# A lightning-attention and MoE kernel on one Trainium2 core: the second group of tokens without Strassen's scheme, weight sums moved to later steps, and the final row stored in parts

## The chip, the cores and the metric

The program runs on one NeuronCore of a Trainium2 chip. The metric is device time in microseconds of one execution, as the median of several. For each kernel one execution was also recorded by the hardware profiler; its span (first to last instruction) is about 1.8 us shorter than the time. Engines are named TensorE (PE in the profile; PEld are its weight loads), VectorE (DVE), ScalarE (ACT), GpSimd (POOL) and SyncE (SP).

## The reference

```python
# attention: B=4, H=8, S=768, D=64, in blocks of 64 rows, decay lam per head
for b in range(nb):
    intra = einsum(qb, kb) * Dmask[None];  intra = einsum(intra, vb)
    inter = einsum(qb * lam_pow, kv_state)
    out[:, :, sl] = intra + inter
    kv_state = lam_block * kv_state + einsum(kb * rev_pow, vb)
# then a dense layer on the 3072 tokens (d_model 512, d_ff 2048)
h = x @ w_in
g = 0.5 * h * (1 + tanh(c * (h + 0.044715 * h**3)))
return g @ w_out
```

Inputs and the output are float32; the matmuls run on float16 copies.

## The kernel before

Attention is done in 24 steps (0 to 23). Its output goes transposed into `xT`, in seven groups of tokens: group 0 has 512, groups 1 and 2 have 256 each, groups 3 to 6 have 512 each. For each group a list of pieces (`filler`) is queued, and `fill(n)` puts the next n pieces between parts of an attention step, so that TensorE always has dense work. A piece of the first layer (`mm1`) ends in a gelu on ScalarE, which writes `gT`. The second layer comes in two forms. `mm2` is the plain one. `product` is Strassen's scheme: seven half-size products in place of eight, for which VectorE makes sums of `gT` blocks (`gs`) and of `w_out` blocks (`w_sum`), and combines the products. Before the change, group 0 is plain and all others use the scheme.

```python
groups = [[0, 1], [2], [3], [4, 5], [6, 7], [8, 9], [10, 11]]
...
def sum_g(i0, i1):                       # five sums of gT on VectorE, one per product that needs one
    for m, ((T0, F0), op, (T1, F1)) in G_SUMS.items():
        if m not in gsum:
            ...                          # pairs live in the ring of four w32 buffers, with the raw weights
        pin(nc.vector.tensor_tensor(gsum[m][:, i, :], block(T0, F0, i), block(T1, F1, i), op))

def product(m, p):
    name, half = PLACE[m]
    if m in (3, 5, 1, 7):
        banks[name] = ps_M.tile([P, 2, HE], FP32, tag="M", name=f"M{name}")
    ...                                  # 8 matmuls of 256 columns into half a bank
    if m == 2:                           # A has 4 and 3, B has 5 and 2
        ...                              # two ScalarE copies of B, then two VectorE adds
    elif m == 1:
        pin(tt(d, banks["C"][:, 0].unsqueeze(1).to_broadcast([P, 2, HE]), d, ALU.add))
    elif m == 6:
        pin(tt(d, banks["D"][:], d, ALU.add))          # D has 7 and 6
        for T in range(2):               # two stores of 256 KB
            ...
...
if g == 0:
    ...                                  # plain
    return
...
for p in range(HN // P):
    for m in (3, 4, 5, 2, 1, 7, 6):
        filler.append(lambda m=m, p=p: product(m, p))
...                                      # sum_g is hung behind certain pieces, in two parts

# the program order around group 1
cast_wout(3, (POOL, ACT))
sum_wout(1, 3, DVE)                      # second half of the weight sums
fill(9)
prep(4)
sum_wout(1, 4, DVE)
stage_t(4)
...
sum_wout(1, 1, DVE)
fill(1); prep(8)
sum_wout(1, 7, POOL)
...
prep(9)
sum_wout(1, 6, POOL)
fill(2)
for n in range(8, NSTEP + 1):
    ...
    fill(2 if n <= 12 else 4)
    R(m, n - 1)                          # scores, products, mask, decay: the attention step
    fill(1)
    U(m)
    fill(2 if n in (8, 11) or n > 12 and n % 2 else 3)
```

## Time and profile before

| | before |
|---|---|
| median time, us | 214.4 (3 runs, 214.19 to 214.74) |
| span of the profiled run, us | 212.6 |
| TensorE busy | 93% |
| VectorE busy | 71% |
| mean granted clock of TensorE | 0.992 |

### The profile page before, as it was taken

How to read it: one execution, taken by the hardware profiler on the slowest of the kernel's cores; microseconds unless marked ns; L12 is line 12 of the kernel's file. 1: busy time of each engine (PE TensorE's matmuls, PEld its weight loads, DVE VectorE, ACT ScalarE, POOL GpSimd, SP SyncE). 2: the span in 40 equal slices, each digit the busy share in tenths (PEclk: the TensorE clock that was granted, in tenths of full speed). 3: DMA queues.
4: the chain of work that ended last, by engine and by line, in shares of the span. 5: the costliest groups of instructions: out<-in, count | busy, mean ns of one | idle time of the engine just before them, and what ended most of it. 6: DMA issues, size and time to landing. Idle time of an engine off the chain costs nothing.

```text
span 212.6 us, 5641 instructions
## 1 busy us (share of the span) xinstructions
PE 197.5 (93%) x2345; PEld 130.4 (61%) x2345; DVE 151.5 (71%) x282; ACT 108.0 (51%) x204; POOL 72.7 (34%) x82
## 2 busy tenths in 40 slices
PE   7788999799992999999999999999999999999990
PEld 2354544356882788855488845588654788445880
DVE  4988529987899978775999727996929773146631
ACT  2364778466770356467742377723376432565110
POOL 5494133646995253342341333044213100000000
PEclk9999999999999699999999999999999999999999
DMA  5999999999969588979695996664450003200022
GB/s 134 299 328 388 384 387 361 284 291 349 335 152 207 121 255 193 179 174 188 159 197 80 295 249 173 51 153 111 99 139 0 3 2 102 99 0 0 3 99 99
DMA packets 64297, 37.85 MB, mean 178 GB/s; under 512 B 17680, under 2 KB 59664, under 8 KB 64272
## 3 DMA queue, kind: packets, MB, share of 16 engines
q1 hardware_dynamic: 64272, 37.50, 68.5%
q8 instruction: 18, 0.29, 0.6%
q14 instruction: 7, 0.06, 0.1%
HBM read 27.27 MB, written 6.29 MB: 158 GB/s over the span
## 4 chain that ended last, share of the span: by engine, by line
PE 72%; DVE 13%; DMA 7%; issue 2%; SPq 2%; ACT 1%; DVEq 0%
PE Hps L401 30%; PE MB L466 8%; PE MD L466 8%; PE MA L466 7%; PE MC L466 4%; DVE w_sum L123 4%; DMA wo<-in_moe_w_out_dram 4%; PE Sps L271 4%; DVE gs L446 3%; PE OK L329 3%; DMA k<-in_k_dram 3%; PE OK L320 2%; PE O2ps L416 2%; SPq L68 2%; DVE qk L221 2%
## 5 line engine op out<-in xcount | busy, mean ns | idle before, releaser
L401 PE MATMUL Hps<-xT,w_in 128*128 128x512 f16 (+1 forms) x416 | 79.1, 346 | 0.0
L405 ACT ACTIVATE gT<-Hps 128x512 f16<-128x512 f32 x88 | 52.5, 596 | 26.4 <-PE Hps L401 25.6
L401 PEld LDWEIGHTS <-w_in 128*128 128x128 f16 x416 | 40.2, 98 | 33.3
L373 POOL TENSOR_TENSOR u<-t,lumask 128x256 f16<-128x256 f32 x40 | 29.3, 739 | 85.1 <-DVE t L366 65.6
L446 DVE TENSOR_TENSOR gs<-gT 128x512 f16<-128x512 f16 (+1 forms) x80 | 45.0, 627 | 11.8 <-ACT gT L405 11.6
L466 PEld LDWEIGHTS <-gs 128*128 128x128 f16 x400 | 39.1, 99 | 8.8 <-DVE gs L446 4.1
L280 DVE TENSOR_TENSOR PT<-Sps,mask 128x1024 f16<-128x1024 f32 x24 | 29.2, 1217 | 17.2 <-PE Sps L271 17.2
L211 POOL TENSOR_TENSOR v<-v,dv 128x512 f16<-128x512 f32 x24 | 29.1, 1214 | 4.8 <-DMA v<-in_v_dram 3.5
L343 ACT ACTIVATE xT<-OK 128x256 f16<-128x256 f32 x48 | 18.2, 452 | 20.0 <-PE OK L329 16.0
L473 ACT ACTIVATE m<-MB 128x512 f32<-128x512 f32 x10 | 6.0, 597 | 35.1 <-PE MB L466 35.1
L466 PE MATMUL MB<-w_out,gs 128*128 128x256 f16 x160 | 19.8, 277 | 3.8 <-DVE gs L446 3.8
L466 PE MATMUL MD<-w_sum,gs 128*128 128x256 f16 x160 | 20.2, 273 | 0.0
L226 ACT ACTIVATE qk<-k 128x512 f16<-128x512 f32 x24 | 15.0, 624 | 9.6 <-DMA k<-in_k_dram 9.6
L466 PE MATMUL MA<-w_sum,gT 128*128 128x256 f16 x160 | 19.5, 273 | 0.1
L221 DVE TENSOR_TENSOR qk<-q,dq 128x512 f16<-128x512 f32 x23 | 17.7, 768 | 0.0
L466 PEld LDWEIGHTS <-gT 128*128 128x128 f16 x160 | 15.5, 98 | 3.1 <-ACT gT L405 0.5
L477 DVE TENSOR_TENSOR o<-MA,m 128x512 f32<-128x512 f32 x10 | 6.9, 688 | 14.5 <-ACT m L473 14.5
L366 DVE SCALAR_TENSOR_TENSOR t<-t,lamu,OK 128x64 f32<-128x64 f32 x64 | 14.5, 273 | 2.1 <-PE OK L306 0.9
L416 PE MATMUL O2ps<-w_out,gT 128*128 128x512 f16 x64 | 14.6, 379 | 0.0
L271 PEld LDWEIGHTS <-qkT 64*64 64x64 f16 x384 | 6.3, 108 | 8.9 <-issue 4.4
L271 PE MATMUL Sps<-qkT 64*64 64x128 f16 x384 | 10.2, 226 | 1.0 <-DVE qkT L247 0.5
L123 DVE TENSOR_TENSOR w_sum<-wo,wo 128x1024 f16<-128x1024 f32 x6 | 8.0, 1362 | 4.2 <-DMA wo<-in_moe_w_out_dram 4.2
(53 smaller groups left out, 168.8 us busy)
## 6 DMA issues: line engine op xcount, KB each, us to landing
q<-in_q_dram SPq DMA_DIRECT2D x24, 256.0 KB, 4.4
k<-in_k_dram SPq DMA_DIRECT2D x24, 256.0 KB, 4.9
v<-in_v_dram SPq DMA_DIRECT2D x24, 256.0 KB, 5.0
out_dram<-o SPq DMA_DIRECT2D x24, 256.0 KB, 3.3
wo<-in_moe_w_out_dram SPq DMA_DIRECT2D x4, 1024.0 KB, 9.1
wi<-in_moe_w_in_dram SPq DMA_DIRECT2D x4, 512.0 KB, 7.7
wi<-in_moe_w_in_dram SPq DMA_DIRECT2D x2, 1024.0 KB, 12.2
qkT<-qk SPq DMA_TRANSPOSE x15, 4.1
```

The costliest lines, as they stand in the source:

```text
L123: pin(eng.tensor_tensor(w_sum16[:, w_slot[m], 4 * j : 4 * j + 4, :], a[:, :, e0 * HE : e0 * HE + HE], b[:, :, e1 * HE : e1 * HE + HE], op))
L211: pin(nc.gpsimd.tensor_tensor(wide(tv[:]), ld32[s][2][:], decay(dv, s), ALU.mult))
L221: pin(q_eng.tensor_tensor(wide(tq), q32[:], decay(dq, s), ALU.mult))
L271: pin(nc.tensor.matmul(Sps[half64(c), hl, hp, jk, :], o[half64(hl), 1, jk, hp, half64(c)], o[half64(hl), 0, :, hp, half64(c)], start=True, ...
L280: pin(nc.vector.tensor_tensor(t[:].rearrange("p a b c d -> p (a b) (c d)"), Ss.pop(n)[:].rearrange("p a b c d -> p (a b) (c d)"), mask[:]. ...
L343: pin(nc.scalar.activation(out=dst[:, :, c * P : (c + 1) * P].rearrange("p hp (t j) -> p hp j t", j=2), in_=OK[c][:, 0:256].rearrange("p ( ...
L373: pin(nc.gpsimd.tensor_tensor(u[:], state[half][:].unsqueeze(2).to_broadcast([P, 2, 2, D]), lumask[:, 2 * half : 2 * half + 2, :].unsqueez ...
L401: pin(nc.tensor.matmul(by_block(Hps[:, i, :]), w_in16[:, c, f * P : (f + 1) * P], x(c), start=(c == 0), stop=(c == NC - 1)))
L405: pin(nc.scalar.activation(out=dst, in_=Hps[:], func=AF.Gelu_apprx_tanh))
L416: pin(nc.tensor.matmul(O2[tau][0][:], gT[:, f % HF, f // HF, tau * P : (tau + 1) * P], w_out16[:, f, :], start=(n == 0), stop=(n == NF - 1)))
L446: pin(nc.vector.tensor_tensor(gsum[m][:, i, :], block(T0, F0, i), block(T1, F1, i), op))
L466: pin(nc.tensor.matmul(dst, lhsT, rhs, start=(i == 0), stop=(i == HF - 1), skip_group_check=True))
```

## The change

The intent: group 1 comes while VectorE has the least room, and its `gs` sums hold up TensorE. Group 1 goes back to the plain form, which needs no sums. Then the second half of the weight sums is first needed by group 2, so those five sums leave the crowded stretch and are done on VectorE in steps 8 to 10. Separately, the last row of the output is stored in three parts, each as soon as it is done.

```diff
+            final = g == len(groups) - 1 and p == HN // P - 1
+            if final and m == 6:
+                name = "E"
-            if m in (3, 5, 1, 7):
+            if m in (3, 5, 1, 7) or name == "E":
...
+            elif final and m in (7, 6):
+                o, T = banks["o"], (0 if m == 7 else 1)
+                row = row0 + T * HN + p * P
+                rows = out[row : row + P, :].rearrange("q (e d) -> q e d", e=2)
+                if m == 7:
+                    low = row0 + HN + p * P
+                    pin(nc.sync.dma_start(out=out[low : low + P, 0:HE], in_=o[:, 0, 1, :]))
+                d = o[:, T, T, :]
+                pin(tt(d, banks[name][:, half], d, ALU.add))
+                if m == 7:
+                    pin(nc.scalar.dma_start(out=rows, in_=o[:, :, 0, :]))
+                else:
+                    pin(nc.sync.dma_start(out=rows[:, 1], in_=d))
...
+        if g == 1:
+            for tau in range(NTAU):
+                for part in (0, 2, 1, 3):
+                    filler.append(lambda tau=tau, part=part: mm2(tau, part))
+            return
...
-    sum_wout(1, 3, DVE)
-    sum_wout(1, 4, DVE)
-    sum_wout(1, 1, DVE)
-    sum_wout(1, 7, POOL)
-    sum_wout(1, 6, POOL)
...
-        fill(2 if n in (8, 11) or n > 12 and n % 2 else 3)
+        for p in {8: (3, 4), 9: (1, 7), 10: (6,)}.get(n, ()):
+            sum_wout(1, p, DVE)
+        fill(2 if n == 11 or n > 12 and n % 2 else 3)
```

## The prediction

> **What bounds the kernel now.** I began with the page: the busy shares and the 40 slices.
>
> ```profile
> PE 197.5 (93%) x2345; PEld 130.4 (61%) x2345; DVE 151.5 (71%) x282; ACT 108.0 (51%) x204; POOL 72.7 (34%) x82
> ...
> PE   7788999799992999999999999999999999999990
> ...
> PEclk9999999999999699999999999999999999999999
> ```
>
> TensorE is busy for 93% of a span of 212.6 us, so the kernel as a whole is bound by its matmuls. But one slice near 64 to 69 us falls to 2, and the next one has a clock of 6 tenths. The waits of TensorE, asked first for the stretch 38 to 92 us and then for 92 us to the end, say how much can be won:
>
> ```profile
> PE MB L466 <- DVE gs L446: 3.8, 1, 3.8
> PE Tps L242 <- DVE qk L221: 1.3, 1, 1.3
> PE Sps L271 <- DVE qkT L251: 0.3, 1, 0.3
> ```
>
> (total us, times, longest). After 92 us the answer is empty: from there to the tail only the number of matmuls counts, and any time won before 92 us is kept unless it runs into a transfer. The timeline of VectorE and GpSimd around the long wait shows its cause:
>
> ```profile
> 60.49 5.61 DVE L446 TENSOR_TENSOR gs<-gT 128x512 f16<-128x512 f16 x5
> 66.02 1.21 DVE L280 TENSOR_TENSOR PT<-Sps,mask 128x1024 f16<-128x1024 f32 x1
> 67.16 0.84 DVE L366 SCALAR_TENSOR_TENSOR t<-t,lamu,OK 128x64 f32<-128x64 f32 x4
> 67.92 3.27 DVE L446 TENSOR_TENSOR gs<-gT 128x512 f16<-128x512 f16 x5
> ...
> 56.06 2.36 POOL L123 TENSOR_TENSOR w_sum<-wo 128x1024 f16<-128x1024 f32 x1
> ...
> 61.43 2.54 POOL L123 TENSOR_TENSOR w_sum<-wo 128x1024 f16<-128x1024 f32 x1
> ```
>
> Five sums of gT for group 1 (the second group of tokens) take 5.6 us, while their median is 0.42 us. One of them lasts 2.57 us, from 61.67 us, beside the 2.54 us GpSimd weight sum. The second five start only at 67.92 us, and TensorE, which has done half of product 5, waits for the first of them. Windows of one microsecond then show the granted clock:
>
> ```profile
> 69.50:70.50 1.00, 1.00 (x6) 0.51 (x4) 1.00 (x2) 0.00 (x0) 0.74 (x1) 0.50 1.13 272
> 70.50:71.50 1.00, 1.00 (x45) 0.89 (x48) 1.00 (x4) 0.78 (x2) 0.00 (x0) 0.50 0.00 0
> 71.50:72.50 1.00, 1.00 (x22) 0.77 (x15) 1.00 (x3) 0.33 (x2) 0.00 (x0) 0.50 0.00 0
> ```
>
> The figure after the five engines is the clock: 0.50 for some 3 us after the stall, so the stall is paid for twice.
>
> **What the skill says.** (1) "SBUF — State Buffer", § Who interferes with whom: a VectorE instruction with two SBUF inputs contends with a GpSimd instruction that reads SBUF. The trace agrees: 2.57 us for a sum whose median is 0.42, beside the GpSimd sum. (2) "TensorE: Matmul & The Clock Gate", Part 1: after about 3.4 us idle the clock falls to half, and about as much work brings it back. The trace agrees: a 3.79 us gap, then 0.50. (3) "VectorE: DVE Perf Modes", § The TRN2 errata: an fp32 tensor_tensor takes (N+151)/0.96 ns; N=1024 gives 1.22 us, and the undisturbed weight sums took 1.21 to 1.22. (4) "SBUF — State Buffer", § The DMA setup-cost knee: a transfer pays about 2 us that do not depend on its size. The last 256 KB stores land 2.5 to 2.6 us after issue, which fits.
>
> **The change part by part.**
>
> *Group 1 loses Strassen's scheme.* Removed: 7 products of 8 matmuls of 256 columns. A run of 8 takes 0.873 us (MA x8, 0.87 in the chain), so 7 x 0.873 = 6.11 us. Added: 2 tiles of 16 matmuls of 512 columns; a run of 8 takes 1.73 us (O2ps x8), so 4 x 1.73 = 6.92 us. On TensorE the change costs **+0.8 us**, all on the path. What it buys is that these matmuls need only gT from ScalarE: the ten gs sums (8.9 us of VectorE in this stretch) and the four combining adds (4 x 0.68) go away. ScalarE gets two copies of 0.60 us instead of 0.60 + 0.38; it is 51% busy, so nothing.
>
> So the wait on gs goes: **-3.79 us**. The slow clock goes too. From 68.64 to 73.56 us TensorE did 12 matmuls of MB, one attention step, and 8 of MC. At full clock this is 12 x 0.109 + 1.03 (the same step from 84.42 to 85.45) + 0.87 = 3.21 us instead of 4.92: **-1.7 us**.
>
> *Weight sums moved.* Five sums of the second half (products 3, 4, 1 on VectorE, 7 and 6 on GpSimd) become five VectorE sums in steps 8 to 10, where group 2 is their first reader. Two of the old ones stood ahead of the first attention preparation, around 38.74 us (2.05 us) and 42.16; that preparation's qk ended at 42.23, and TensorE waited 1.30 us for it although its earlier work ended at 40.99. Without the sum, qk can run from 38.74 to about 39.7, and k is done at 40.05 (ScalarE, 39.42 + 0.63), both before TensorE is free: **-1.3 us**. The sum of 1.25 us at 52.93 stood ahead of the copy for which TensorE waited at 55.86: **-0.3 us**.
>
> The new places cost VectorE 2.4, 2.4 and 1.2 us. My estimate of a step from the same matmul pieces: one attention step 0.93, six pieces of 0.87, together 6.1 us. VectorE has in step 8: mask 1.22, decay about 0.9, sums 2.44, next q 0.68, together 5.3 us; step 9 the same; in step 10: 0.68 + 1.22 + 0.9 + 1.22 and the first five gs sums of group 2 (2.6), together 6.6. That last is over by 0.5 us, but before, group 2 had product 5 start at 86.16 with its first sums done at 83.17 and the second at 85.9, and the second half of the product needs them only after 86.6. I take this for hidden. The staging buffers are reused in a ring of four, and gs of group 2 now takes the ones of the weights; all their readers are in order on VectorE ahead of it, so no new wait.
>
> *The final row.* Before: the last matmul ends near 207.3, an add of 128x512 runs from 207.42 to 208.11, and SP issues two stores of 256 KB from 208.14 to 209.34, one after the other. The second is issued at about 208.7 and lands 2.5 us later; the span ends 1.4 us after that. After: the product 7 half is added first. It stands behind the MC add (begun 206.64, spacing 0.60), so at about 207.24; at (256+151)/0.96 = 0.42 us each, with about 0.33 us between starts, the last add ends near 208.0. The last store of 128 KB is issued then, at once, with the 256 KB row store 0.3 us ahead of it on ScalarE's queue and the third store long gone. Last issue 208.0 instead of 208.7, and a little less to move behind it: **-0.9 us**.
>
> **Sum:** +0.8 - 3.8 - 1.7 - 1.3 - 0.3 - 0.9 = -7.2 us, and 214.4 - 7.2 = 207.2. I add 0.1 for small new waits: **207.3 us**.
>
> **The rivals.**
>
> *The wait moves to group 2.* VectorE is late with the five sums, so gs of group 2 makes TensorE wait. For: step 10 is slightly over full, and GpSimd's v and u work can stretch a 1.22 us sum to 2 (it did at 38.74, 2.05). Against: VectorE loses some 16 us of work between 38 and 76 us (8.9 gs, 2.7 adds, 4.5 of sums) and gets 6.1 back, and GpSimd loses 4.9. It would give back 1 to 3 us; a gap over 3.4 us would also bring back the slow clock, and the time would be near 212.
>
> *DMA becomes the bound from 38 to 65 us.* For: the DMA share there is 1.0 to 1.1 at 280 to 350 GB/s, k for step 5 was waited for until 42.06, and the 7 us won mean that the same bytes must come sooner. Against: later loads were not waited for at all in this stretch, they are asked for three steps ahead, and land in about 5 us. It would take back 0.5 to 2 us: 208 to 209.5.
>
> *The gap was partly hidden.* If something else, such as the transposing transfer for the next step, had stopped TensorE soon after in any case, less than 5.5 us comes back. Against: after the stall no wait of TensorE is left in the trace, although it then ran close behind its inputs.
>
> *The stores in parts wait for each other.* If the row's parts were ordered as one buffer, the last add would wait 2.5 us for a store to have read it. The parts are disjoint, so I give this little; it would make the tail 2 us longer.
>
> **Range and chances.** The stall with its slow clock (5.5) is the safest term; the 0.8 is sure; the 1.3 and 0.9 could each be half. The best case without losses is about 206.0; a new wait of 2 us gives 209.3. Range 206.0 to 209.3. Faster by over 2% means below about 210.2; that fails only if a new wait of 3 us appears: 0.91. Within 2%: 0.08. Slower: 0.01.
>
> **What would show it.** The waits of TensorE between 38 and 92 us should be empty or under 0.5 us; the clock 1.00 in every slice after the start; O2ps matmuls rise from 64 to 96 and those on gs fall from 400 to 360; the first preparation's transposes start at 41.0 instead of 42.3; TensorE ends near 201 us instead of 207.3; the time from its end to the span's end shrinks from 5.3 to about 4.4 us. A wait of MB on gs near 78 us, or one on qkT or k, would make the prediction wrong.

## More of the kernel before

The 71% of VectorE is an average. The windows view of the kernel before, in stretches of 4 us, gives the length of the stretch, then for each engine busy us and, in brackets, the number of instructions, in the order PE, PEld, DVE, ACT, POOL; then the granted clock, the DMA share and GB/s:

```profile
58.00:62.00 4.00, 4.00 (x85) 3.44 (x83) 3.90 (x7) 3.18 (x7) 4.00 (x5) 1.00 0.63 141
62.00:66.00 4.00, 2.85 (x26) 2.14 (x23) 4.00 (x4) 1.40 (x3) 3.15 (x2) 1.00 1.39 228
66.00:70.00 4.00, 1.36 (x10) 1.14 (x11) 4.00 (x9) 0.00 (x0) 2.31 (x3) 0.93 0.84 206
70.00:74.00 4.00, 4.00 (x70) 3.08 (x68) 4.00 (x7) 1.64 (x4) 0.24 (x1) 0.65 0.36 77
```

VectorE is the third figure pair: 15.9 of 16 us. Where TensorE stands still (2.85 and 1.36 of 4 us), VectorE is full, and in 62 to 66 us it gets through only four instructions, beside a sum on GpSimd.

## The result, and the profile after

| | before | after |
|---|---|---|
| median time, us | 214.57 (4 runs, 214.19 to 215.48) | 207.5 (4 runs, 207.16 to 209.66) |
| span of the profiled run, us | 212.6 | 205.6 |
| last matmul ends, us | 207.39 | 200.57 |
| from there to the end, us | 5.21 | 5.03 |
| TensorE busy | 93% | 96% |
| mean granted clock over the span | 0.992 | 1.000 |

The ratio is 0.9686, with a 95% interval of 0.9613 to 0.9759. A ratio is the mean time of one kernel's fast runs over that of the other's fast runs of the same rounds, so it is not quite the ratio of the medians quoted here. One of the four runs of the kernel after, 209.66 us with a mean clock of 0.990, is apart from the other three (207.16 to 207.61). It has no trace, and its cause is open.

The page of the kernel after has the same three rows as were shown of before: the busy shares, TensorE in 40 slices, and the granted clock.

```profile
PE 197.1 (96%) x2321; PEld 128.0 (62%) x2321; DVE 144.4 (70%) x271; ACT 108.1 (53%) x204; POOL 69.9 (34%) x80
...
PE   7988999999999999999999999999999999999990
...
PEclk9999999999999999999999999999999999999999
```

The dip and the slow slice are gone. TensorE's waits over the whole execution (total us, times, longest) are these:

```profile
PE idle L573 <- DVE ones L144: 1.5, 1, 1.5
PE Hps L514 <- DVE w_in L107: 0.8, 1, 0.8
PE Sps L271 <- DVE qkT L247: 0.5, 1, 0.5
PE Tps L242 <- DVE qk L221: 0.3, 1, 0.3
PE OK L320 <- DVE t L366: 0.2, 1, 0.2
```

All five also come up when only the first 21 us are asked for. The stretch from 36 to 86 us, and that from 86 us to the end, list none. So the three waits that the prediction listed are gone, and none has taken their place.

VectorE, however, has not become free. The windows of the kernel after, one for each attention step from step 8 on and the last for step 11, have the same columns as above:

```profile
58.70:64.80 6.10, 6.10 (x79) 3.38 (x78) 5.99 (x9) 3.08 (x6) 5.21 (x4) 1.00 1.25 241
64.80:71.00 6.20, 6.20 (x89) 4.28 (x88) 6.20 (x9) 2.96 (x6) 4.06 (x4) 1.00 1.12 274
71.00:77.50 6.50, 6.44 (x93) 5.44 (x92) 6.50 (x11) 4.76 (x10) 2.94 (x3) 1.00 1.12 247
77.50:82.90 5.40, 5.40 (x85) 4.66 (x84) 4.71 (x11) 2.16 (x5) 1.53 (x2) 1.00 0.90 155
```

VectorE is busy for 18.7 of the 18.8 us of steps 8 to 10. It is full and TensorE still never waits for it. How near that is to a new stall is a question for the experiments.

At the tail, the timeline of the kernel before shows one add for both halves and two stores, issued one after the other:

```profile
207.42 0.69 DVE L484 TENSOR_TENSOR o<-MD,o 128x512 f32<-128x512 f32 x1
208.14 1.20 SPq L487 DMA_DIRECT2D out_dram<-o  x2
```

and that of the kernel after has two adds and three stores, the first of them (not shown) at 199.93:

```profile
199.53 1.04 PE L469 MATMUL ME<-w_sum,gs 128*128 128x256 f16 x8
199.82 0.68 DVE L484 TENSOR_TENSOR o<-MC,o 128x512 f32<-128x512 f32 x1
...
200.61 0.42 DVE L494 TENSOR_TENSOR o<-MD,o 128x256 f32<-128x256 f32 x1
200.95 0.41 DVE L494 TENSOR_TENSOR o<-ME,o 128x256 f32<-128x256 f32 x1
201.06 0.64 ACTq L496 DMA_DIRECT2D out_dram<-o  x1
201.39 0.36 SPq L498 DMA_DIRECT2D out_dram<-o  x1
```

The matmuls of product 7 are done near 199.7, but its add begins at 200.61: 0.79 us after the start of the add ahead of it, whose result it reads (it is also 0.04 us after the end of the last matmul, 200.57; the run with another order of products, below, tells the two apart). The last add ends 0.79 us after the last matmul (201.36 against 200.57). Before it was 0.72 (208.11 against 207.39). The parts have not brought the last add forward at all.

### The profile page after: what moved, and what is told of

The parts are those of the page before. It is cut to its first block, busy times and chain, and to the rows that moved or that the text cites. A ratio compares the mean times of both kernels' runs of the same rounds, so it can differ in the third digit from the quotient of the medians.

```text
span 205.6 us, 5583 instructions
## 1 busy us (share of the span) xinstructions
PE 197.1 (96%) x2321; PEld 128.0 (62%) x2321; DVE 144.4 (70%) x271; ACT 108.1 (53%) x204; POOL 69.9 (34%) x80
## 4 chain that ended last, share of the span: by engine, by line
PE 91%; DVE 2%; DMA 2%; issue 1%; ACT 1%; DVEq 0%
PE Hps L401 35%; PE O2ps L416 10%; PE MB L469 8%; PE MA L469 7%; PE MD L469 7%; PE Sps L271 4%; PE MC L469 4%; PE Hps L514 4%; PE OK L329 3%; PE idle L573 3%; PE OK L320 3%; PE Tps L242 2%; DMA qkT<-qk 2%; PE OK L306 1%; DVE t L366 1%
## 5 line engine op out<-in xcount | busy, mean ns | idle before, releaser
L373 POOL TENSOR_TENSOR u<-t,lumask 128x256 f16<-128x256 f32 x40 | 31.4, 791 | 80.9 <-DVE t L366 54.2
L446 DVE TENSOR_TENSOR gs<-gT 128x512 f16<-128x512 f16 (+1 forms) x70 | 36.6, 586 | 10.8 <-ACT gT L405 10.6
L469 PEld LDWEIGHTS <-gs 128*128 128x128 f16 x360 | 34.9, 98 | 4.0
L416 PE MATMUL O2ps<-w_out,gT 128*128 128x512 f16 x96 | 21.9, 379 | 0.0
L221 DVE TENSOR_TENSOR qk<-q,dq 128x512 f16<-128x512 f32 x23 | 19.2, 834 | 0.0
L469 PE MATMUL MA<-w_sum,gT 128*128 128x256 f16 x144 | 17.5, 273 | 0.1
L469 PE MATMUL MD<-w_sum,gs 128*128 128x256 f16 x136 | 17.5, 273 | 0.0
L469 PE MATMUL MB<-w_out,gs 128*128 128x256 f16 x144 | 17.2, 273 | 0.0
L480 DVE TENSOR_TENSOR o<-MA,m 128x512 f32<-128x512 f32 x9 | 6.2, 688 | 13.9 <-ACT m L476 13.9
L469 PEld LDWEIGHTS <-gT 128*128 128x128 f16 x144 | 14.0, 98 | 2.8 <-ACT gT L405 0.3
L416 PEld LDWEIGHTS <-gT 128*128 128x128 f16 x96 | 9.2, 98 | 9.9
```

Of the source, the lines that this page charges most:

```text
L221: pin(q_eng.tensor_tensor(wide(tq), q32[:], decay(dq, s), ALU.mult))
L373: pin(nc.gpsimd.tensor_tensor(u[:], state[half][:].unsqueeze(2).to_broadcast([P, 2, 2, D]), lumask[:, 2 * half : 2 * half + 2, :].unsqueez ...
L416: pin(nc.tensor.matmul(O2[tau][0][:], gT[:, f % HF, f // HF, tau * P : (tau + 1) * P], w_out16[:, f, :], start=(n == 0), stop=(n == NF - 1)))
L469: pin(nc.tensor.matmul(dst, lhsT, rhs, start=(i == 0), stop=(i == HF - 1), skip_group_check=True))
```

## The experiments

Three questions were open. What did each part bring? Was the stall caused by contention with GpSimd or by the amount of VectorE's work, and what did the slow clock cost by itself? And why did the tail give 0.2 us and not 0.9? All runs gave correct results. The kernel before was run again on the chip of each set: 214.63, 214.44 and 215.18 us (medians of 11 runs each). Times from the last matmul to the end are good to 0.05 us, as the spans are given to 0.1; the first expectation writes 5.29 and 5.05 us for what is 5.21 and 5.03 here.

### The parts by themselves

**Only the final row in parts** (the kernel before with the tail edits of the diff above and nothing else).

> The kernel before with only the final row stored in parts. My prediction gave this part 0.9 us. The trace of the changed kernel speaks for less: from the end of the matmuls to the end of the span it has 5.05 us against 5.29 before. Theory (the last adds are chained on VectorE, so that the last store is not issued earlier; only the second issue and some bytes are saved, and the end of the program costs a little more with a second store queue): 0.2 to 0.4 us faster than before, the stall of 3.8 us unchanged. Rival (0.9 is right and the one trace is an accident): 0.8 to 1.0 us faster, with 4.4 us from the last matmul to the end.

Measured: 213.58 us against 214.63. This can't be read from the times, because the runs of before on this chip go from 212.86 to 215.51 (see below). In the trace it has 4.63 us from the last matmul to the end against 5.21, and the stall of 3.8 us is there as before. That 0.6 us lies between the two theories. Runs of like mean clock on this chip say about the same: three of before at 0.990 to 0.992 have 214.25 to 214.49, five of this one at 0.991 to 0.992 have 213.48 to 214.30, with medians 0.7 us apart.

**Everything but the final row in parts** (the changed kernel without the tail edits).

> The changed kernel with the old way of storing the final row. If the tail is worth 0.2 to 0.4 us, this is 0.2 to 0.4 us slower than the changed kernel, 6.5 to 6.9 us faster than before, and about 5.3 us from the last matmul to the end. If it is worth 0.9, it is only 6.1 us faster than before.

Measured: 207.52 us (6 runs, 207.17 to 207.79), ratio 0.9669, and 5.03 us from the last matmul to the end. The changed kernel has 207.5 us and 5.03 us as well. Between these two the tail edit is worth nothing that shows. Over all traces with the old tail (before, this one, and three experiments below) the time from the last matmul to the end is 5.21, 5.03, 5.01, 5.16 and 5.18, mean 5.12. Over those with the new tail (after, its repeat, tail only, and three experiments below) it is 5.03, 4.99, 4.63, 5.05, 5.02 and 5.07, mean 4.97. The means differ by 0.15 us, and by 0.09 without the trace of the tail alone. So the edit is worth nothing in one pair of kernels and 0.6 to 0.7 us in the other; the section on the prediction takes this up.

**Only group 1 made plain**, with the weight sums left in their old places:

```diff
+        if g == 1:
+            for tau in range(NTAU):
+                for part in (0, 2, 1, 3):
+                    filler.append(lambda tau=tau, part=part: mm2(tau, part))
+            return
-        fill(2 if n in (8, 11) or n > 12 and n % 2 else 3)
+        fill(2 if n == 11 or n > 12 and n % 2 else 3)
```

> The kernel before with only the second group of tokens made dense; the weight sums stay where they were, two on GpSimd. Theory (my terms: stall 3.79 and slow clock 1.71 go, 0.81 of matmuls is added, the waits of 1.30 and 0.32 us for VectorE sums at 42 and 56 us stay): 4.7 us faster than before, TensorE waits of 1.3 and 0.3 us still there, clock 1.00. Rival (the moved sums were needed to take the stall away, because GpSimd's two long sums hold up VectorE just there): a wait of 1 us or more remains between 60 and 75 us and the gain is below 4 us.

Measured: 209.5 us, 5.1 us below the median of before (ratio 0.9761, from 0.9722 to 0.9801, so "unclear" by the 2% rule, but clearly faster). Its TensorE waits between 30 and 60 us are the two that the sums cause, and there is none later:

```profile
PE Tps L242 <- DVE qk L221: 1.1, 1, 1.1
PE Sps L271 <- DVE qkT L251: 0.3, 1, 0.3
```

So the stall goes even with the two GpSimd sums in place: plain matmuls read nothing that VectorE makes. Moving the sums is worth the rest, 209.5 - 207.52 = 2.0 us. The prediction had 1.3 + 0.3 for it.

### What the stall was made of

**Matmuls of ones in the gap** (the kernel before, with TensorE kept busy while it waits):

```diff
+        if g == 1:
+            k5 = len(filler) - 5
+            five = filler[k5]
+            filler[k5] = lambda: (idle(16), five())
```

> The kernel before with 16 matmuls of ones (16 x 0.216 = 3.45 us at full clock) put into the gap in which TensorE waits for the sums of gT; nothing else is changed and the sums come no earlier. Theory (the slow clock after the gap is a cost of its own of 1.7 us): the clock stays at 1.00 and the kernel is 1.7 us faster than before although it does 3.5 us more of matmuls. Rival (after the gap TensorE would be held by VectorE's sums anyway, so that the clock costs nothing): same time as before within 0.4 us, with new waits on the sums or the mask.

Measured: 212.91 us against 214.63, which is 1.7 us faster although TensorE does 3.5 us more. In its timeline the matmuls of ones fill the gap, and product 5 goes on at 68.62 where it went on at 68.64 before:

```profile
64.23 3.62 PE L555 MATMUL idle<-ones 128*128 128x512 f16 x16
67.69 0.60 PE L466 MATMUL MB<-w_out,gs 128*128 128x256 f16 x4
68.62 1.49 PE L466 MATMUL MB<-w_out,gs 128*128 128x256 f16 x12 [0.34 <-DVE gs L446]
```

and its windows after the gap have the clock at 1.00:

```profile
70.00:72.00 2.00, 2.00 (x63) 1.77 (x63) 2.00 (x5) 1.64 (x4) 0.22 (x1) 1.00 0.25 61
```

The next attention step starts 1.55 us earlier than before (76.31 against 77.86). The slow clock is a cost of its own.

The same cost explains a part of the spread of the kernel before. Sorted by the mean clock, its 33 runs in the three sets fall into classes:

| mean clock | runs | time, us |
|---|---|---|
| 0.998 | 2 | 212.72 to 212.86 |
| 0.990 to 0.992 | 11 | 214.12 to 214.55 |
| 0.985 to 0.986 | 6 | 214.18 to 214.66 |
| 0.977 to 0.978 | 14 | 215.02 to 216.18 |

(The one of 216.18 counts as slow by being over 1.5% above the fastest; it is not in the ratios.) The two runs that kept the clock are as fast as the kernel with the gap filled. This correlation covers all 33 runs; I did not control what decides how long the slow phase lasts. The mean clock is a rough guide, though, as it also counts the time after the last matmul: the trace of the kernel with only group 1 plain has a mean of 0.995, yet in its windows the clock is below 1.00 only from 205 us on, and its last matmul ends at 202.79. That may be why the two middle classes have the same times; no trace of the class at 0.985 was kept.

**The two GpSimd sums on VectorE** (the kernel before; `sum_wout(1, 7, POOL)` and `sum_wout(1, 6, POOL)` with `DVE`).

> The kernel before with only one thing changed: the two weight sums that GpSimd did at 56 and 61 us are done by VectorE at the same places of the program. Theory (the stall comes from too much VectorE work in front of the second five sums of gT; the contention with GpSimd is only a part): VectorE gets 2.4 us more and gives back about 3 us of stretched sums, so the second five begin 0 to 1 us earlier, TensorE still waits 2.8 to 4 us, and the time is 0 to 1 us better (up to 2.5 if the gap becomes short enough that the clock stays up). Rival (the contention with GpSimd is the stall): the wait falls below 1 us and the time is 4 us or more better.

Measured: 213.61 us against 214.44, 0.8 us faster, at the edge of the noise (ratio 0.9965, from 0.9929 to 1.0). With GpSimd's long sums gone, the first five `gs` sums do take 2.60 us in place of 5.61. But the two sums now stand in VectorE's own queue, and the second five start later than before, at 68.39 (67.92 before):

```profile
66.76 0.60 PE L466 MATMUL MB<-w_out,gs 128*128 128x256 f16 x4
69.09 1.48 PE L466 MATMUL MB<-w_out,gs 128*128 128x256 f16 x12 [1.72 <-DVE gs L446]
...
63.94 2.60 DVE L446 TENSOR_TENSOR gs<-gT 128x512 f16<-128x512 f16 x5
...
68.39 3.25 DVE L446 TENSOR_TENSOR gs<-gT 128x512 f16<-128x512 f16 x5
```

Product 5 goes on at 69.09, 0.45 us later than before. The wait of 1.72 us is shorter only because TensorE now also waits 2.3 us for a copy of qkT near 58 us. In this run the two shorter stops leave the clock at 1.00 in every window from 64 to 76 us, and the first-layer piece after the products starts at 74.05 where it was 75.14: the 0.45 us lost are won back with 1.1 us to spare by the faster matmuls. (Its three other runs have mean clocks of 0.986 to 0.991 and no trace, so whether the clock stayed up in them is not shown. The two runs of before that kept the clock, 212.72 and 212.86, are faster than this one's 213.40.) My expectation that the second five would start 0 to 1 us earlier missed. The rival (contention is the stall) misses by far more: what fills VectorE is the amount of work, and moving it between the two engines only moves the stop.

### The price of leaving the scheme out, and the room that is left

**Group 2 made plain too** (`if g in (1, 2):`).

> The changed kernel with the third group of tokens (256 tokens too) made dense as well. No wait of TensorE stands there any more, so this measures the price of leaving out the scheme by itself. Theory: 32 x 0.216 - 56 x 0.109 = 0.81 us, all on the path: 0.7 to 0.9 us slower than the changed kernel. Rival (the scheme's price on VectorE still delays something hidden): same time or faster.

Measured: 208.15 us (207.69 to 209.67) against 207.5 of the changed kernel, 0.65 us slower and slightly below the range. The trace says how much. Its attention step near 71 us starts 0.30 us late by the start of the run (71.34 against 71.04), and its last matmul ends 0.86 us late (201.43 against 200.57), so the edit costs 0.56 us of TensorE's time. In the changed kernel, the first product of group 2 takes longer than its 1.04:

```profile
76.34 1.27 PE L469 MATMUL MA<-w_sum,gT 128*128 128x256 f16 x8
```

It needs the last gelu of its group at once, while the plain form starts with older ones. If that is the cause, which no run here shows, these 0.23 us come back, and 0.81 - 0.23 = 0.58.

**Two of the moved sums done twice** (`{8: (3, 4), 9: (1, 7, 7), 10: (6, 6)}`), run beside the unaltered changed kernel.

> The changed kernel, unaltered, on the same chip as the next three, as their measure. 207.2 to 207.7 us; from the last matmul to the end 4.8 to 5.1 us.

> The changed kernel with two of the moved weight sums done twice (the same values written again), one more in step 9 and one more in step 10: 2.4 us more of VectorE work ahead of group 2's sums of gT. Theory (VectorE is full from 59 to 77 us in the changed kernel, 18.7 of 18.8 us, and the second half of product 5 has only about 1.4 us of room): TensorE waits about 1 us for the sums of gT near 80 us, and the kernel is 0.7 to 1.5 us slower than the changed kernel. Rival (there is ample room, as my prediction had it with 5.3 us of work in steps of 6.1): no wait, same time within 0.2 us.

Measured: the changed kernel again has 207.43 us, and this one 208.53, 1.1 us slower. The stall is back, at group 2:

```profile
79.39 0.60 PE L469 MATMUL MB<-w_out,gs 128*128 128x256 f16 x4
80.74 1.48 PE L469 MATMUL MB<-w_out,gs 128*128 128x256 f16 x12 [0.75 <-DVE gs L446]
```

So by my estimate (2.4 us of work added, a wait of 0.75 us) the changed kernel stands 1 to 2 us of VectorE work away from the same stall, one group later.

**The sums for products 7 and 6 on GpSimd**, in the same steps 9 and 10 (`POOL if p in (7, 6) else DVE`).

> The changed kernel with the moved sums for products 7 and 6 on GpSimd instead of VectorE, at the same places in steps 9 and 10. Theory (the engine does not matter here as long as group 2's sums come in time, and GpSimd's long sums stretch VectorE's by about what they save it): time within 0.4 us of the changed kernel, perhaps a wait of up to 1 us on the sums of gT near 80 us. Rival (having the sums on VectorE is a part of the gain): 1.5 us or more slower.

Measured: 207.42 us against 207.43, and no TensorE wait after 36 us. The five `gs` sums of group 2 take 4.82 us beside GpSimd's sum of 2.53 us, but VectorE has 1.66 us of idle time before, so they still come in time. That the sums are on VectorE is not a part of the gain. That they stand later is.

### The tail

**All three stores of the final row on SP** (`nc.scalar.dma_start` for the row becomes `nc.sync.dma_start`).

> The changed kernel with the row store of the final row issued on SP like the other two, not on ScalarE's queue. Theory (a second queue in use costs something at the end of the program: SP's last wait was 2.3 us with it and 1.9 without): the last store is issued 0.3 us later, the end after its landing is 0.3 us shorter, so the same time within 0.15 us. Rival (the second queue is a plain gain): 0.3 us slower from the last matmul to the end.

Measured: 207.26 us, and 4.81 us from the last matmul to the end, with the last store issued at 202.22, which is 1.13 us after the last matmul (201.09) where it was 0.82 on two queues. A later issue did not make the end later. SP's last wait is 1.7 us against 2.3, as expected. But a cost of the second queue at the end of the program is not shown by this: the last store lands 2.2 us after its issue, at 204.4, and the span ends 1.5 us later, as in the changed kernel (201.39 + 2.7 = 204.1, and 205.6). What differs is the landing, 2.2 us in place of 2.7.

**Another order of products in the final row**, 5, 2, 3, 4, 1, 7, 6, so that ScalarE's copies of B are done before A is:

```diff
-            if m == 2:
+            if m == (4 if final else 2):
...
-            for m in (3, 4, 5, 2, 1, 7, 6):
+            for m in ((5, 2, 3, 4, 1, 7, 6) if g == len(groups) - 1 and p == HN // P - 1
+                      else (3, 4, 5, 2, 1, 7, 6)):
```

> The changed kernel with the products of the final row in the order 5, 2, 3, 4, 1, 7, 6, so that ScalarE's two copies run beside products 3 and 4 and the chain of adds on VectorE starts earlier. Theory (the last store is held by the chain of adds, in which each add that reads what the one before wrote starts 0.79 us after it and not 0.60): the last add ends 0.5 us after the last matmul instead of 0.79, and the time from the last matmul to the end is about 0.3 us shorter, 4.5 to 4.7 us. Rival (the end is set by the stores' landing and the program's end alone): no change within 0.1 us. In the time of the whole kernel 0.3 us is at the edge of what five rounds show.

> The version with the other order of products in the final row, once more, beside the changed kernel on one chip. Theory (0.33 us of the chain of adds goes, and the row store has moved its bytes before the last store comes): 0.4 to 0.7 us faster than the changed kernel, last add 0.46 us after the last matmul, end 4.4 to 4.6 us after it. Rival (the 0.6 us seen between two chips was chance): within 0.2 us of the changed kernel.

Measured: 206.83 us, and 206.77 beside the changed kernel's 207.43 on one chip, 0.66 us faster (five of its six runs are below the lowest of the other, the sixth is as slow as its highest); 4.44 and 4.37 us from the last matmul to the end. The timeline of the first of the two:

```profile
199.24 0.68 DVE L484 TENSOR_TENSOR o<-MC,o 128x512 f32<-128x512 f32 x1
...
199.52 1.04 PE L469 MATMUL ME<-w_sum,gs 128*128 128x256 f16 x8
200.03 0.42 DVE L494 TENSOR_TENSOR o<-MD,o 128x256 f32<-128x256 f32 x1
200.48 0.64 ACTq L496 DMA_DIRECT2D out_dram<-o  x1
200.60 0.42 DVE L494 TENSOR_TENSOR o<-ME,o 128x256 f32<-128x256 f32 x1
201.05 0.37 SPq L498 DMA_DIRECT2D out_dram<-o  x1
```

The add of product 7 again starts 0.79 us after the add whose result it reads (199.24, 200.03), this time 0.53 us before the last matmul ends (200.56). So it is the chain that holds it, not the last matmul, and with this order the chain is done sooner. The row store of 256 KB is issued 0.08 us before the last matmul ends (200.48 against 200.56) where it was 0.49 us after it, and the last add ends 0.46 us after the last matmul, where it was 0.79. This version beats both kernels: its ratios to before are 0.9637 and 0.9633.

## Why the prediction was right

**The bound and the size.** The text had 207.3 us, and 207.5 was measured. That it is so near is partly luck: the final row gave 0.7 us less than foretold in the profiled run, and the two waits, a head start and a shorter first product gave 0.5 us more, with 0.1 us set aside for new waits that did not come. The last matmul ends 6.82 us earlier, and the attention steps from 71 us on (77.86 became 71.04, 84.35 became 77.53) already start 6.82 us earlier: everything was won before 72 us and kept to the end, as the empty list of waits after 92 us had promised.

| term | predicted, us | found, us | from |
|---|---|---|---|
| plain matmuls for group 1 | +0.81 | +0.80 | 32 matmuls in 4.32 + 2.59 us against 6.11 |
| wait on gs and slow clock | -5.50 | -5.50 | before: product 5 to the next first-layer piece, 64.25 to 75.14; group 2 in the kernel after: 79.34 to 84.73 |
| wait at 42 us | -1.30 | -1.46 | both timelines, less the head start |
| wait at 56 us | -0.32 | -0.40 | 55.86 became 53.84, of which 1.62 was there already |
| not in the sum: head start of this run; first product of group 1 | 0 | -0.16; -0.10 | 23 matmuls left at 35.71 us against 24 at 35.65; 2.01 against 1.91 for 16 |
| final row | -0.9 | -0.2 | 5.21 to 5.03 |

The found terms without the last add up to -6.82.

**The stall.** The mechanism was as described. That its two halves are separate costs is shown by the gap filled with ones. Which half is how large is not fixed: the slow half is 1.55 us in the profiled run and, if the classes of clock differ in nothing else (which I did not check), from nothing to over 2 us in others. This spread of 3 us is that of the kernel *before*, so it moves the gain, from some 5 to 8 us, and not the time of the kernel after. The chance of missing a gain lay here more than in the places that the prediction named.

**The waits at 42 and 56 us.** They were a little larger than I took them (2.0 us by the runs with and without the moved sums). The first one also varies: five traces with the sums in their old places list it with 1.1 to 1.7 us. And the text misread one line: of the two sums around 38.74 and 42.16 us, only the first stood ahead of qk, which ran from 40.71 to 42.23. The wait view counts from the modelled end of the matmul ahead. In an unbroken stream, the next one starts 0.16 us before that end (in the kernel after, one group ends at 35.71 + 5.13 = 40.84 and the next starts at 40.67), so a stop costs this much more than its entry says.

**The room on VectorE.** The step that failed here without harm was the sum of 5.3 us for a step of 6.1. Measured were 5.99 and 6.20: next to GpSimd the sums took 1.4 to 1.6 us and q 1.53 in place of 0.68. (The text's own example of a stretched sum, 2.05 us at 38.74, ran beside GpSimd's cast of `w_out`, 37.73 to 39.71, and not only beside v.) The conclusion, that group 2 gets its sums in time, held by a small margin, as the run with extra sums shows.

**The final row.** This term was mis-sized, 0.2 us in the profiled runs (from nothing to 0.7 in the other pairs) in place of 0.9. The step that failed was: "It stands behind the MC add (begun 206.64, spacing 0.60), so at about 207.24". The spacing of 0.60 is that of adds that do not read the result of the add just before them. This add reads what the MC add wrote, and it starts 0.79 us after it; so the last add ends at 0.79 us after the last matmul, where I had put it near 208.0, some 0.6 after. The last store was issued 0.82 us after the last matmul, against about 1.3 before, but only 0.2 of these 0.5 us reached the end. The last store's bytes come behind those of the 256 KB row store, issued 0.33 us ahead of it: it lands 2.7 us after its issue, where the first part, also 128 KB but alone, took 1.7. So it lands 3.5 us after the last matmul, against about 3.9 before (1.3 + 2.6). From there to the end it is about 1.1 us in the tail-only trace and in the one without the tail edits, 1.3 in before and 1.5 in after. (These are estimates from issue times and the landing times of the DMA view.) So the store came about 0.4 us earlier, and the end of the program took all of it, a part or none. Why that end differs from kernel to kernel stays open. The run with the other order shows that the chain was the right place to look, as it took away 0.33 us of the chain and issued the row store 0.57 us earlier against the matmuls; the end came 0.6 us earlier.

**The rivals.** The wait did not move to group 2, and DMA did not become the bound (TensorE has no wait at all after 21 us). The gap was not partly hidden: its 5.50 us came back in full. The parts of the row did not wait for each other: the last add starts at 200.95, before the store issued at 199.93 has landed 1.7 us later.

## What to carry to other kernels

A scheme that saves matmuls by adding work to another engine is worth its saving only where that engine has room: here 0.8 us of matmuls saved cost a stop of 3.8 us, because VectorE was full in just that stretch, while its average was 71%. Count a stop of TensorE with what the clock loses after it, and check in the windows view, stretch by stretch, that the helper engine has room; moving the two sums between VectorE and GpSimd made none here. At the end of a kernel, follow the chain of adds that read each other before splitting the stores: the order of the last products brought 0.66 us, and splitting from nothing to 0.7.

## What the Trainium skill lacked or had wrong

- "TensorE: Matmul & The Clock Gate", Part 1, puts the ramp penalty below 1% of a typical kernel's span. It says so of the warm-up at the start of a kernel; here the slow clock after one stop in its middle cost 1.7 us of 214.6, by the run with the gap filled. The page does not say how often a stop near the window's length slows the clock: 31 of 33 runs of the kernel before, with its stop of 3.8 us, had a mean clock of 0.992 or less; of 56 runs of the kernels with no stop of over 1.7 us after the start, one had. (The kernel with both GpSimd sums on VectorE, with stops of 1.7 and 2.3 us, is not counted: three of its four runs had.)
- The same page, § Back-to-back issue gap, gives about 131 ns for a matmul of 512 columns in a real stream of loads and matmuls. No run here shows it: 20 of them took 4.32 us in the kernel after, 0.216 us each, which is its figure for the isolated one.
- No page gives the spacing of two VectorE adds when the second reads what the first wrote. Behind an add of 128x512 fp32 with a record of 0.68 us it was 0.78 to 0.79 us (the two runs with the other order), against 0.60 when the second does not read it.
